# Feed-forward stage: product M4 issued three matmuls later, and the next block's preparation in smaller pieces

## The chip, the cores and the metric

The kernel runs on one core of one Trainium2 chip. The metric is the device time of one execution, in microseconds (us). Before the change the median of three runs is 5206.62 us (5202.1 to 5209.15).

## What is computed

Three layers, each on the output of the one before, in float32. The change touches the last one alone, the feed-forward layer with d_model 256 and d_ff 2048, on 24576 rows:

```python
def _attn_ref(u, v, z):            # 8 batches, 3072 rows, 256 columns
    scores = (1.0 / S) * np.matmul(z, z.transpose(0, 2, 1))
    return u * np.matmul(np.maximum(scores, 0.0) ** 2, v)
...
    x = _moe_ref(x=attn_out.reshape(B * S, D), **moe_kwargs)   # top-1 of 8 experts
...
def _moe2_ref(x, w_in, w_out):
    h = x @ w_in                               # 24576 x 2048
    g = h * (1.0 / (1.0 + np.exp(-h)))
    return (g @ w_out).astype(np.float32)      # 24576 x 256
```

## The kernel before

The program has two pipelines one after the other: `pipeline_ab` (attention and experts, up to about 3190 us) and `pipeline_c` (feed-forward, from there to the end). All orders are written out by hand: within the stage each engine runs its instructions in the order in which Python emits them, and waits only for semaphores.

**Blocks and steps.** `pipeline_c` (L1253 and on) goes through 24 blocks of 1024 rows (CB), each in two halves of 512 rows. A block has 8 steps (GP), one per 2 x 128 hidden columns, so there are 192 steps, numbered g; i = g mod 8 is the step's place in its block. Every float32 product is three matmuls of 128x512 (high by high, high by low, low by high part), emitted by `emit_M` (L1211 to L1213) and `emit_AV_c` (L1237 to L1239).

**One step.** The four quarters H11, H12, H21, H22 of the hidden layer (two column groups by two row halves) are made from seven products M1 to M7 instead of eight, in PSUM banks Q (two, alternating by step), R and Z:
- M1 goes to Q, M2 to R; H11 = Q + R.
- M6 is added onto Q (start=False), so Q must have been copied out first (`copy(0)` before M6, `copy(1)` before M5, `copy(2)` before M3; ScalarE, L1269).
- M7 starts Z; H22 = Z + copy 2.
- M4 is added onto Z, so it must wait until VectorE has read Z for H22 (`add("H22", 2, Z)`, L1272); H21 = Z + copy 1.
- M3 is the last product on Q; H12 is Q itself.

Each quarter then goes through `sig` (ScalarE, L1275, sigmoid), `mul` (VectorE, L1278), `high` (ScalarE, L1284, rounded copy) and `low_part` (VectorE, L1288, the rest), and one step later through `emit_AV_c`, six matmuls with the second weight (three for each of d = 0, 1) into four accumulators. "H12's six matmuls" below means that last part for H12. Some of this falls into the next step: mul H21, high H21 and high H12, and the low parts of H22, H12 and H21.

**TensorE's order in a step** is M1, M2, H11's six, M6, M7, H22's six, M5, H21's six, M3, M4, H12's six: 45 matmuls, where the six-matmul groups belong to the step before.

**VectorE's order** is low H22, low H12, mul H21 (all three of the step before), add H11, low H21, mul H11, the preparation, low H11, add H22, mul H22, add H21, mul H12. **ScalarE's order** is high H12 of the step before, copy 0, high H21, sig H11, copy 1, high H11, the preparation, copy 2, sig H22, sig H12, high H22, sig H21.

**Preparation of the next block.** `prep_c(b)` (L1190) lists what makes the inputs of block b: `load_c` (eight DMAs on SP's queue), two `tr_c` (VectorE transposes of 128x1024, L1158), four `sum_c` (VectorE, 128x512, L1173) and four `parts_c`, each a split: a ScalarE copy (`xp`, L153) and a VectorE subtraction that waits for it (L154), 128x1024 for three of them and 128x512 for the fourth. Before the change one entry of the list is emitted in the middle of each step: the load at i=1, both transposes at i=2, two sums at i=3, two at i=4, the three large splits at i=5, 6 and 7, the small split at i=0 of the block itself.

**Output.** At i=0 the accumulators of the block before are read by four VectorE transposes (`evac_c`, L1245), each pair followed by four stores on SP's queue.

Of the kernel before, what the change touches and what calls it, by code (L numbers as in the profile page):

```python
# [20 lines left out]
def relu2_attention__moe_top1__silu_ffn_kernel(  # L21
# [60 lines left out]
    NCB = N // CB  # L82
    GP = DFF // P // 2
# [874 lines left out]
    for b in range(NBLK):  # L958
        g = NIT + b * FP
# [191 lines left out]
    def load_c(b):  # L1151
        for t in range(2):
            XC[t] = mt("y", [P, CH // 32, 64], F32, "xc", t)
            load_rows(XC[t], CH // P, X2[b * CB + t * CH:b * CB + (t + 1) * CH])

    def tr_c(b, t):
        o = TC[t] = mt("u", [P, KD, CH], F32, "xs", t)
        V.transpose(out=o.rearrange("p k (j c) -> p j k c", c=32),  # L1158
                    in_=XC[t].rearrange("p j (r k) -> p j k r", k=KD))

    def sum_c(n):

        if n == 0:
            TC[2] = mt("y", [P, KD, CH], F32, "xs", 0)
            o, x, y = TC[2][:, 0], TC[1][:, 0], TC[0][:, 0]
        elif n == 1:
            o, x, y = TC[1][:, 0], TC[1][:, 1], TC[1][:, 0]
        elif n == 2:
            o, x, y = TC[2][:, 1], TC[1][:, 1], TC[2][:, 0]
        else:  # L1170
            TC[3] = mt("y", [P, CH], F32, "xs", 1)
            o, x, y = TC[3], TC[0][:, 1], TC[2][:, 1]
        V.tensor_tensor(out=o, in0=x, in1=y, op=ALU.subtract)  # L1173

    def parts_c(b, n):

        if n == 3:
            h, l = (mt("st", [P, CH], F32R, "xp", x) for x in range(2))
        elif n == 1:
            h, l = (mt("a" if b % 2 == 0 else "xh", [P, KD, CH], F32R, "xp") for x in range(2))  # L1180
        else:
            h, l = (mt("w2" if n else "xl", [P, KD, CH], F32R, "xp", 2 * (n and b % 2) + x) for x in range(2))
        split(h, l, TC[n])
        if n == 3:
            XF["T4"] = h, l
        else:
            for k, name in enumerate((("B11", "B21"), ("T3", "B22"), ("T1", "T2"))[n]):
                XF[b % 2 if n else 0, name] = h[:, k], l[:, k]

    def prep_c(b):  # L1190

        return [[], [lambda: load_c(b)], [lambda: tr_c(b, 0), lambda: tr_c(b, 1)],
                [lambda: sum_c(0), lambda: sum_c(1)], [lambda: sum_c(2), lambda: sum_c(3)],
                [lambda: parts_c(b, 1)], [lambda: parts_c(b, 2)], [lambda: parts_c(b, 0)], [lambda: parts_c(b, 3)]]

    FACTORS = dict(M1=("A11", "B11"), M2=("A12", "B21"), M3=("S4", "B22"), M4=("A22", "T4"), M5=("S1", "T1"),
                   M6=("S2", "T2"), M7=("S3", "T3"))
# [8 lines left out]
    def emit_M(g, name, o, start=True):  # L1206
        b, i = divmod(g, GP)
        w, x = FACTORS[name]
        wh, wl = (a[:, i * P:(i + 1) * P] for a in weights_c(w))
        xh, xl = XF[x if x == "T4" else (0 if x in ("B11", "B21") else b % 2, x)]  # L1210
        T.matmul(o, lhsT=wh, rhs=xh, start=start, stop=False, skip_group_check=True)  # L1211
        T.matmul(o, lhsT=wh, rhs=xl, start=False, stop=False, skip_group_check=True)  # L1212
        T.matmul(o, lhsT=wl, rhs=xh, start=False, stop=True, skip_group_check=True)  # L1213

    QUADS = dict(H11=(0, 0), H22=(1, 1), H21=(1, 0), H12=(0, 1))
    quads, acc_c, out_c, room = {}, {}, {}, {}
# [5 lines left out]
        room["c"] = [*(mt("st", [P, CH], F32, "c", 6 + i) for i in range(2)), x[:, 0]]  # L1222
        room["a"] = {q: mt("st", [P, CH], F32, "sg", 2 + i) for i, q in enumerate(QUADS)}

    def emit_AV_c(g, q):

        b, i = divmod(g, GP)
        f, t = QUADS[q]
        x = quads.pop((g, q))
        start = i == 0 and q in ("H11", "H22")  # L1230
        stop = i == GP - 1 and q in ("H21", "H12")
        for d in range(2):
            if start:
                acc_c[b, d, t] = cw["ps"].tile([P, CH], F32, tag=f"acc{2 * t + d}", name="acc", bufs=1)
            o = acc_c[b, d, t]
            wh, wl = (cw["o"][:, f * GP + i, y, d * P:(d + 1) * P] for y in range(2))
            T.matmul(o, lhsT=wh, rhs=x[:, 0], start=start, stop=False)  # L1237
            T.matmul(o, lhsT=wh, rhs=x[:, 1], start=False, stop=False)  # L1238
            T.matmul(o, lhsT=wl, rhs=x[:, 0], start=False, stop=stop)  # L1239

    def evac_c(b, t, d):
        if d == 0:
            out_c[t] = mt("u", [P, CH // 32, 64], F32, "oc", t)
        o = out_c[t]
        V.transpose(out=o.rearrange("p j (r k) -> p j k r", k=2)[:, :, d],  # L1245
                    in_=acc_c.pop((b, d, t)).rearrange("p (j c) -> p j c", c=32))
        if d == 1:
            rows = out[b * CB + t * CH:b * CB + (t + 1) * CH]
            for i in range(4):
                SP.dma_start(out=rows[:, 64 * i:64 * i + 64].rearrange("(j c) m -> c j m", c=32),  # L1250
                             in_=o[32 * i:32 * i + 32])

    def pipeline_c():  # L1253
        not_c.close()
        ps = cw["ps"] = ctx.enter_context(tc.tile_pool(name="psC", bufs=1, space=PSUM))
        banks = [ps.tile([P, CH], F32, tag=f"m{i}", name="m", bufs=1) for i in range(4)]
        ns = NCB * GP
        rooms_c()
        n_quad = 0
        H, C, S = room["H"], room["c"], room["a"]  # L1260
        for g in range(ns + 1):
            now, old = g < ns, g > 0
            b, i = divmod(g, GP)
            end = old and i == 0
            todo = prep_c(b)[GP] if now and i == 0 else prep_c(b + 1)[i] if now and b + 1 < NCB else []
            Q, R, Z = banks[g % 2], banks[2], banks[3]

            def copy(n, src):
                A.activation(out=C[n], in_=src, func=AF.Copy)  # L1269

            def add(q, n, src):
                V.tensor_tensor(out=H[q], in0=src, in1=C[n], op=ALU.add)  # L1272

            def sig(q, src=None):
                A.activation(out=S[q], in_=H[q] if src is None else src, func=AF.Sigmoid)  # L1275

            def mul(q, src=None):
                V.tensor_tensor(out=S[q], in0=H[q] if src is None else src, in1=S[q], op=ALU.mult)  # L1278

            def high(g, q):  # L1280
                nonlocal n_quad
                quads[g, q] = mt("hl"[n_quad % 2], [P, 2, CH], F32R, "g")
                n_quad += 1
                A.activation(out=quads[g, q][:, 0], in_=S[q], func=AF.Copy)  # L1284

            def low_part(g, q):
                x = quads[g, q]
                V.tensor_tensor(out=x[:, 1], in0=S[q], in1=x[:, 0].bitcast(F32), op=ALU.subtract)  # L1288

            if now:  # L1290
                emit_M(g, "M1", Q)
            if old:
                high(g - 1, "H12")
                low_part(g - 1, "H22")
            if now:
                copy(0, Q)
                emit_M(g, "M2", R)
            if old:
                low_part(g - 1, "H12")
                mul("H21")  # L1300
                high(g - 1, "H21")
            if now:
                add("H11", 0, R)
            if old:
                low_part(g - 1, "H21")
                emit_AV_c(g - 1, "H11")
            if now:
                sig("H11")
                mul("H11")
                emit_M(g, "M6", Q, False)  # L1310
                copy(1, Q)
                high(g, "H11")
                emit_M(g, "M7", Z)
            for fn in todo:
                fn()
            if now:
                low_part(g, "H11")
            if old:
                emit_AV_c(g - 1, "H22")
            if now:  # L1320
                emit_M(g, "M5", Q, False)
                copy(2, Q)
            if old:
                emit_AV_c(g - 1, "H21")
            if now:
                add("H22", 2, Z)
                sig("H22")
                emit_M(g, "M3", Q, False)
                emit_M(g, "M4", Z, False)
            if end:  # L1330
                evac_c(b - 1, 0, 0)
            if now:
                sig("H12", Q)
                mul("H22")
                high(g, "H22")
            if end:
                evac_c(b - 1, 0, 1)
            if now:
                add("H21", 1, Z)
                mul("H12", Q)  # L1340
                sig("H21")
            if old:
                emit_AV_c(g - 1, "H12")
            if end:
                for d in range(2):
                    evac_c(b - 1, 1, d)

    with tc.manual_schedule():
        start_a()
# [48 lines left out]
```

## Time and profile before

| | |
|---|---|
| median of 3 runs | 5206.62 us (5202.1 to 5209.15) |
| the profiled execution's own time | 5207.61 us |
| its span, first to last instruction | 5205.9 us |
| busy over the span: TensorE, VectorE, ScalarE, GpSimd | 99%, 77%, 67%, 15% |
| feed-forward stage | from about 3198 us to the end |
| granted TensorE clock, mean | 0.996 of full |

All timeline rows are of one execution and give the start and duration of an instruction, and in brackets how long its engine stood idle just before it and what ended that. TensorE's matmuls overlap: each is shown 0.39 us long, but in an undisturbed stretch the next one begins about 0.227 us after the one before, so the busy share says little, and gaps are read from starts. The profiled execution is 1.0 us above the median of the runs.

### The profile page before, as it was taken

The page shows a single profiled execution, that of the slowest core. Times are in us where ns is not written, and L with a number is a line of the kernel's source. Part 1 is how long each engine was busy: PE and PEld are TensorE (multiplying, and loading weights), DVE is VectorE, ACT ScalarE, POOL GpSimd, SP SyncE. Part 2 cuts the span into 40 slices and gives each one's busy share as a digit, 9 for nine tenths or more (in the row PEclk, how much of TensorE's full clock was granted, in tenths as well). Part 3 has the DMA queues.
Part 4 walks back from the last instruction along what each step waited for, and adds up shares of the span by engine and source line. Part 5 has one row for each costly group of instructions (what it writes and reads, how often), then busy time and mean ns, then how long its engine had stood idle before and what let it go on. Part 6 is the DMA issues. An engine that isn't in the chain of part 4 may idle for free.

```text
span 5205.9 us, 76118 instructions
## 1 busy us (share of the span) xinstructions
PE 5130.2 (99%) x27488; PEld 4403.7 (85%) x27488; DVE 4016.5 (77%) x5760; ACT 3501.9 (67%) x5213; POOL 759.3 (15%) x977
## 2 busy tenths in 40 slices
PE   8999999999999999999999998999999999999999
PEld 7999888888989898888888887888888888888887
DVE  6687777777777778778877667888887888888787
ACT  7787777777777776555555555666666666666666
POOL 1131313131323221311111111000000000000000
PEclk9999999999999999999999999999999999999999
DMA  4555555556565556755555543011010101101010
GB/s 150 179 169 177 175 181 166 180 168 190 166 179 166 181 168 191 192 161 159 162 153 154 162 141 115 21 28 33 17 33 17 33 21 29 33 17 33 17 33 17
DMA packets 789371, 594.31 MB, mean 114 GB/s; under 512 B 473692, under 2 KB 706175, under 8 KB 788992
## 3 DMA queue, kind: packets, MB, share of 16 engines
q1 hardware_dynamic: 616960, 464.93, 30.2%
q10 hardware_dynamic: 152928, 73.95, 5.6%
q0 software_dynamic: 19104, 50.56, 2.6%
q8 instruction: 215, 3.52, 0.3%
q14 instruction: 164, 1.34, 0.1%
HBM read 368.03 MB, written 210.73 MB: 111 GB/s over the span
## 4 chain that ended last, share of the span: by engine, by line
PE 68%; issue 9%; DVE 8%; ACT 8%; DMA 6%; POOL 1%; SPq 1%; ACTq 0%; POOLq 0%; DVEq 0%
PE acc L244 6%; PE acc L241 6%; PE acc L1239 5%; PE acc L1237 5%; PE acc L1238 5%; PE m L1211 4%; PE m L1213 4%; PE m L1212 4%; PE acct L702 4%; PE acct L703 4%; PE acct L704 4%; PE acc L243 3%; PE acc L242 3%; ACT g L1284 2%; PE s L647 2%
## 5 line engine op out<-in xcount | busy, mean ns | idle before, releaser
L1284 ACT ACTIVATE g<-sg 128x512 fp32r<-128x512 f32 x768 | 485.8, 633 | 222.5 <-DVE sg L1278 209.3
L1237 PE MATMUL acc<-g,wo 128*128 128x512 f32 x1536 | 598.5, 390 | 0.0
L1238 PE MATMUL acc<-g,wo 128*128 128x512 f32 x1536 | 597.9, 389 | 0.2 <-DVE g L1288 0.2
L1239 PE MATMUL acc<-g,wo 128*128 128x512 f32 x1536 | 597.9, 389 | 0.0
L1288 DVE TENSOR_TENSOR g<-sg,g 128x512 fp32r<-128x512 f32 x768 | 524.5, 685 | 58.0 <-ACT g L1284 22.0
L702 PE MATMUL acct<-vs,th 128*128 128x256 f32 x1920 | 542.7, 283 | 5.5 <-DVE rt L509 5.5
L703 PE MATMUL acct<-vs,th 128*128 128x256 f32 x1920 | 542.3, 282 | 0.0
L704 PE MATMUL acct<-vs,tl 128*128 128x256 f32 x1920 | 542.1, 282 | 0.0
L244 PE MATMUL acc<-vs,ah 128*128 128x512 f32 x1344 | 533.3, 397 | 0.0
L241 PE MATMUL acc<-vs,ah 128*128 128x512 f32 x1344 | 532.8, 396 | 0.0
L1275 ACT ACTIVATE sg<-hs 128x512 f32<-128x512 f32 x576 | 364.4, 633 | 216.0 <-DVE hs L1272 206.7
L669 DVE TENSOR_TENSOR al<-a,ah 128x1024 fp32r<-128x1024 f32 x336 | 409.9, 1220 | 108.2 <-ACT ah L662 108.0
L1278 DVE TENSOR_TENSOR sg<-hs,sg 128x512 f32<-128x512 f32 x576 | 395.6, 687 | 120.4 <-ACT sg L1275 118.6
L656 ACT ACTIVATE a<-s 128x1024 f32<-128x1024 f32 x336 | 342.2, 1018 | 183.8 <-PE s L648 160.6
L932 ACT ACTIVATE hh<-hps 128x1024 fp32r<-128x1024 f32 (+1 forms) x220 | 213.7, 971 | 348.4 <-PE hps L918 344.1
L933 DVE SCALAR_TENSOR_TENSOR hl<-hps,hh 128x1024 fp32r<-128x1024 f32 (+1 forms) x220 | 254.0, 1155 | 208.1 <-ACT hh L932 207.5
L681 ACT ACTIVATE th<-at 128x1024 fp32r<-128x1024 f32 x240 | 253.4, 1056 | 224.3 <-PE acct L703 139.7
L667 DVE STREAM_TRANSPOSE tb<-a 128x1024 f32<-128x1024 f32 x240 | 297.5, 1240 | 128.5 <-ACT a L658 125.0
L243 PE MATMUL acc<-vs,al 128*128 128x256 f32 x1344 | 375.4, 279 | 0.0
L703 PEld LDWEIGHTS acct<-vs,th 128*128 128x128 f32 x1920 | 366.1, 191 | 10.4
L242 PE MATMUL acc<-vs,al 128*128 128x256 f32 x1344 | 374.0, 278 | 0.0
L702 PEld LDWEIGHTS acct<-vs,th 128*128 128x128 f32 x1920 | 365.4, 190 | 7.8 <-DVE rt L509 7.8
(246 smaller groups left out, 13978.7 us busy)
## 6 DMA issues: line engine op xcount, KB each, us to landing
ts_scratch<-tb SPq DMA_DIRECT2D x240, 512.0 KB, 3.4
at<-ts_scratch SPq DMA_DIRECT2D x960, 128.0 KB, 2.8
r<-in_moe_w_dram SPq DMA_DIRECT2D x220, 512.0 KB, 5.0
vr<-in_v_dram ACTq DMA_DIRECT2D x48, 512.0 KB, 4.8
ut<-in_u_dram ACTq DMA_DIRECT2D x48, 512.0 KB, 4.5
xb<-xs_scratch SPq DMA_DIRECT2D x192, 128.0 KB, 2.6
xc<-x_scratch SPq DMA_DIRECT2D x192, 128.0 KB, 2.5
out_dram<-oc SPq DMA_DIRECT2D x192, 128.0 KB, 2.0
```

Source lines behind the costliest of these rows:

```text
L241: T.matmul(acc, lhsT=hs[0], rhs=ws[0], start=start, stop=False)
L242: T.matmul(acc[:, D:2 * D], lhsT=ls[0], rhs=ws[0][:, 0:D], start=False, stop=False)
L243: T.matmul(acc[:, D:2 * D], lhsT=ls[1], rhs=ws[1][:, 0:D], start=False, stop=False)
L244: T.matmul(acc, lhsT=hs[1], rhs=ws[1], start=False, stop=stop)
L702: T.matmul(acc[:, kk], lhsT=lh, rhs=vq[:, 0], start=(q == 0), stop=False)
L703: T.matmul(acc[:, kk], lhsT=lh, rhs=vq[:, 1], start=False, stop=False)
L704: T.matmul(acc[:, kk], lhsT=ll, rhs=vq[:, 0], start=False, stop=(q == QT - 1))
L1237: T.matmul(o, lhsT=wh, rhs=x[:, 0], start=start, stop=False)
L1238: T.matmul(o, lhsT=wh, rhs=x[:, 1], start=False, stop=False)
L1239: T.matmul(o, lhsT=wl, rhs=x[:, 0], start=False, stop=stop)
L1284: A.activation(out=quads[g, q][:, 0], in_=S[q], func=AF.Copy)
L1288: V.tensor_tensor(out=x[:, 1], in0=S[q], in1=x[:, 0].bitcast(F32), op=ALU.subtract)
```

## The change

M4 moves behind the first three of H12's six matmuls; `emit_AV_c` gets an argument `half` for that. On VectorE mul H12 now stands ahead of add H21. The preparation list gets two entries a step: the even one at the old place in the middle of the step, the odd one at the step's end. The load of a block's input goes to i=0 of the block before it.

```diff
     def prep_c(b):
-        return [[], [lambda: load_c(b)], [lambda: tr_c(b, 0), lambda: tr_c(b, 1)],
-                [lambda: sum_c(0), lambda: sum_c(1)], [lambda: sum_c(2), lambda: sum_c(3)],
-                [lambda: parts_c(b, 1)], [lambda: parts_c(b, 2)], [lambda: parts_c(b, 0)], [lambda: parts_c(b, 3)]]
+        none = lambda: None
+        return [none, none, lambda: tr_c(b, 0), none, lambda: tr_c(b, 1), none, lambda: sum_c(0), lambda: sum_c(1),
+                lambda: sum_c(2), lambda: sum_c(3), lambda: parts_c(b, 1), none, lambda: parts_c(b, 2), none,
+                lambda: parts_c(b, 0), none, lambda: parts_c(b, 3)]
...
-    def emit_AV_c(g, q):
+    def emit_AV_c(g, q, half=None):
...
-        x = quads.pop((g, q))
+        x = quads[g, q] if half == 0 else quads.pop((g, q))
...
-        for d in range(2):
+        for d in range(2) if half is None else (half,):
...
-            for fn in todo:
-                fn()
+            if now and i == 0:
+                prep_c(b)[2 * GP]()
+                if later:
+                    load_c(b + 1)
+            if later:
+                prep_c(b + 1)[2 * i]()
...
                 emit_M(g, "M3", Q, False)
+            if old:
+                emit_AV_c(g - 1, "H12", 0)
+            if now:
                 emit_M(g, "M4", Z, False)
...
             if now:
+                mul("H12", Q)
                 add("H21", 1, Z)
-                mul("H12", Q)
                 sig("H21")
             if old:
-                emit_AV_c(g - 1, "H12")
+                emit_AV_c(g - 1, "H12", 1)
             if end:
                 for d in range(2):
                     evac_c(b - 1, 1, d)
+            if later:
+                prep_c(b + 1)[2 * i + 1]()
```

The line numbers of the changed kernel are one higher than before from L1211 on. The following rows are each engine's own order around the end of step i=5 and the start of i=6 of one block. Names: sg_35720, 35721, 35722, 35723 hold H11, H22, H21 and H12 after sigmoid; m_35715 is Z, m_35712 and m_35713 are the two Q; c_35718 and c_35719 are copy 0 and copy 1; hs_35716 holds copy 2 and then H21.

VectorE before, from low H11 of step 5 to low H21 in step 6:

```order
L1288 TENSOR_TENSOR g_49787<-sg_35720,g_49787 128x512
L1272 TENSOR_TENSOR hs_35717<-m_35715,hs_35716 128x512
L1278 TENSOR_TENSOR sg_35721<-hs_35717,sg_35721 128x512
L1272 TENSOR_TENSOR hs_35716<-m_35715,c_35719 128x512
L1278 TENSOR_TENSOR sg_35723<-m_35713,sg_35723 128x512
L1288 TENSOR_TENSOR g_49823<-sg_35721,g_49823 128x512
L1288 TENSOR_TENSOR g_49837<-sg_35723,g_49837 128x512
L1278 TENSOR_TENSOR sg_35722<-hs_35716,sg_35722 128x512
L1272 TENSOR_TENSOR hs_35717<-m_35714,c_35718 128x512
L1288 TENSOR_TENSOR g_49846<-sg_35722,g_49846 128x512
```

VectorE after, the same piece:

```order
L1289 TENSOR_TENSOR g_49787<-sg_35720,g_49787 128x512
L1273 TENSOR_TENSOR hs_35717<-m_35715,hs_35716 128x512
L1279 TENSOR_TENSOR sg_35721<-hs_35717,sg_35721 128x512
L1279 TENSOR_TENSOR sg_35723<-m_35713,sg_35723 128x512
L1273 TENSOR_TENSOR hs_35716<-m_35715,c_35719 128x512
L1289 TENSOR_TENSOR g_49826<-sg_35721,g_49826 128x512
L1289 TENSOR_TENSOR g_49837<-sg_35723,g_49837 128x512
L1279 TENSOR_TENSOR sg_35722<-hs_35716,sg_35722 128x512
L1273 TENSOR_TENSOR hs_35717<-m_35714,c_35718 128x512
L1289 TENSOR_TENSOR g_49846<-sg_35722,g_49846 128x512
```

Rows four and five changed places: mul H12 (sg_35723) is now ahead of add H21 (hs_35716); nothing else moved there.

ScalarE after, from copy 2 of step 6 to high H21 in step 7, the same as before but for line numbers and buffer names:

```order
L1270 ACTIVATE hs_35716<-m_35712 128x512
L1276 ACTIVATE sg_35721<-hs_35717 128x512
L1276 ACTIVATE sg_35723<-m_35712 128x512
L1285 ACTIVATE g_49901<-sg_35721 128x512
L1276 ACTIVATE sg_35722<-hs_35716 128x512
L1285 ACTIVATE g_49912<-sg_35723 128x512
L1270 ACTIVATE c_35718<-m_35713 128x512
L1285 ACTIVATE g_49921<-sg_35722 128x512
```

Here nothing moved: sig H21 (sg_35722) still stands ahead of high H12 (g from sg_35723), and copy 0 of the next step behind both.

TensorE before, from the last of H21's matmuls to M1 of the next step, one step:

```order
L1239 MATMUL acc_50093<-g_50444,wo_24244 128x512
L1211 MATMUL m_35712<-xp_49792,s4_35601 128x512
L1212 MATMUL m_35712<-xp_49793,s4_35601 128x512
L1213 MATMUL m_35712<-xp_49792,s4_35602 128x512
L1211 MATMUL m_35715<-xp_50017,wih_24242 128x512
L1212 MATMUL m_35715<-xp_50018,wih_24242 128x512
L1213 MATMUL m_35715<-xp_50017,wil_24243 128x512
L1237 MATMUL acc_50109<-g_50435,wo_24244 128x512
L1238 MATMUL acc_50109<-g_50435,wo_24244 128x512
L1239 MATMUL acc_50109<-g_50435,wo_24244 128x512
L1237 MATMUL acc_50113<-g_50435,wo_24244 128x512
```

TensorE after, the same piece:

```order
L1240 MATMUL acc_50093<-g_50444,wo_24244 128x512
L1212 MATMUL m_35712<-xp_49792,s4_35601 128x512
L1213 MATMUL m_35712<-xp_49793,s4_35601 128x512
L1214 MATMUL m_35712<-xp_49792,s4_35602 128x512
L1238 MATMUL acc_50109<-g_50435,wo_24244 128x512
L1239 MATMUL acc_50109<-g_50435,wo_24244 128x512
L1240 MATMUL acc_50109<-g_50435,wo_24244 128x512
L1212 MATMUL m_35715<-xp_50017,wih_24242 128x512
L1213 MATMUL m_35715<-xp_50018,wih_24242 128x512
L1214 MATMUL m_35715<-xp_50017,wil_24243 128x512
L1238 MATMUL acc_50113<-g_50435,wo_24244 128x512
```

M4, the three matmuls into m_35715 (Z), now follows the first three of H12's six matmuls instead of M3 (into m_35712).

## Rows read from the trace of the kernel before

**Rows 1.** Waits, whole feed-forward stage: who waited for whom: us in total, times, longest.
```profile
PEld m L1211 <- DVE hs L1272: 35.1, 70, 0.9
```

**Rows 2.** Timeline of TensorE: M3 to M4 at i=5 and 6; M5 at i=1.
```profile
4009.29 0.39 PE L1213 MATMUL m<-xp,s 128*128 128x512 f32 x1
4009.61 0.50 PE L1211 MATMUL m<-xp,wih 128*128 128x512 f32 x1
4009.94 0.39 PE L1212 MATMUL m<-xp,wih 128*128 128x512 f32 x1
...
4019.73 0.39 PE L1213 MATMUL m<-xp,s 128*128 128x512 f32 x1
4020.26 0.50 PE L1211 MATMUL m<-xp,wih 128*128 128x512 f32 x1
...
4048.51 0.39 PE L1239 MATMUL acc<-g,wo 128*128 128x512 f32 x1
4048.78 0.50 PE L1211 MATMUL m<-xp,wih 128*128 128x512 f32 x1
```

**Rows 3.** Timeline of VectorE, i=3, 4 and 5 of the next block.
```profile
4070.88 0.69 DVE L1272 TENSOR_TENSOR hs<-m,hs 128x512 f32<-128x512 f32 x1 [0.96 <-ACT hs L1269]
...
4081.08 0.69 DVE L1272 TENSOR_TENSOR hs<-m,hs 128x512 f32<-128x512 f32 x1 [0.96 <-ACT hs L1269]
...
4083.11 0.69 DVE L1272 TENSOR_TENSOR hs<-m,c 128x512 f32<-128x512 f32 x1
...
4091.78 0.68 DVE L1272 TENSOR_TENSOR hs<-m,hs 128x512 f32<-128x512 f32 x1
```

**Rows 4.** Timeline of VectorE, add H22 of i=5 to add H22 of i=0.
```profile
4008.87 0.68 DVE L1272 TENSOR_TENSOR hs<-m,hs 128x512 f32<-128x512 f32 x1
4010.25 0.69 DVE L1278 TENSOR_TENSOR sg<-hs,sg 128x512 f32<-128x512 f32 x1 [0.70 <-ACT sg L1275]
4010.86 0.68 DVE L1272 TENSOR_TENSOR hs<-m,c 128x512 f32<-128x512 f32 x1
4011.46 0.68 DVE L1278 TENSOR_TENSOR sg<-m,sg 128x512 f32<-128x512 f32 x1
4012.05 1.47 DVE L1288 TENSOR_TENSOR g<-sg,g 128x512 fp32r<-128x512 f32 x2
...
4019.52 0.68 DVE L1272 TENSOR_TENSOR hs<-m,hs 128x512 f32<-128x512 f32 x1
...
4030.17 0.68 DVE L1272 TENSOR_TENSOR hs<-m,hs 128x512 f32<-128x512 f32 x1
...
4039.25 0.68 DVE L1288 TENSOR_TENSOR g<-sg,g 128x512 fp32r<-128x512 f32 x1
4040.10 0.69 DVE L1272 TENSOR_TENSOR hs<-m,hs 128x512 f32<-128x512 f32 x1 [0.17 <-ACT hs L1269]
```

**Rows 5.** Timeline of ScalarE: sig H21, high H12, copy 0 after i=5; high H12 after i=4.
```profile
4011.63 0.63 ACT L1275 ACTIVATE sg<-hs 128x512 f32<-128x512 f32 x1
4012.17 0.63 ACT L1284 ACTIVATE g<-sg 128x512 fp32r<-128x512 f32 x1
4012.71 0.58 ACT L1269 ACTIVATE c<-m 128x512 f32<-128x512 f32 x1
...
4084.44 0.63 ACT L1284 ACTIVATE g<-sg 128x512 fp32r<-128x512 f32 x1
```

**Rows 6.** Timeline of VectorE, i=2: the two transposes of the preparation.
```profile
4057.71 2.36 DVE L1158 STREAM_TRANSPOSE xs<-xc 128x1024 f32<-128x1024 f32 x2
```

**Rows 7.** The page's DMA issues: operation, count, size of each, us from issue to landing.
```profile
xc<-x_scratch SPq DMA_DIRECT2D x192, 128.0 KB, 2.5
out_dram<-oc SPq DMA_DIRECT2D x192, 128.0 KB, 2.0
```

**Rows 8.** Windows: busy us (count) of PE, PEld, DVE, ACT, POOL; PEclk; DMA share, GB/s.
```profile
3197.90:3210.00 12.10, 6.49 (x13) 3.90 (x14) 8.71 (x10) 4.03 (x7) 0.00 (x0) 0.52 0.07 17
...
4007.25:4089.92 82.67, 82.38 (x360) 67.07 (x359) 67.16 (x102) 55.73 (x92) 0.00 (x0) 1.00 0.11 26
```

More of the change, by code (lines that the diff above doesn't have):

```diff
@@ L1264, in pipeline_c @@
             end = old and i == 0
-            todo = prep_c(b)[GP] if now and i == 0 else prep_c(b + 1)[i] if now and b + 1 < NCB else []
+            later = now and b + 1 < NCB
             Q, R, Z = banks[g % 2], banks[2], banks[3]
```

## The prediction, made before the changed kernel was run

> **What bounds the kernel now.** I began with the page's busy shares (TensorE 99%) and the waits of the feed-forward stage, the only stage that the change touches. There one entry stops TensorE again and again: a weight load of the first matmul of a product waits for VectorE's add, 70 times, 35.1 us in all [rows 1]. 70 is three for each of 23 blocks, and one.
>
> Then the timeline of TensorE. Its undisturbed spacing is 0.227 us, so a step of 45 matmuls takes 10.20 us; the same 10.20 lies between the add H22 of i=3 and of i=4 (4070.88 to 4081.08), both of which wait 0.96 us for copy 2, thus for TensorE's M5 [rows 3]. A block, taken from the add H22 of i=5 to the next one (4008.87 to 4091.78), is 82.91 us [rows 3, 4]. Eight undisturbed steps are 81.60, so 1.31 us a block are lost. The reader finds them in four places [rows 2]: M4 at i=5 begins 0.32 us after M3's last matmul (0.09 late), and the matmul behind it follows at 0.33 instead of 0.227, a restart of 0.11: 0.20 together. At i=6 the gap is 0.53, so 0.30 and 0.11; i=7 is the same. M5 at i=1 begins 0.27 after its predecessor: 0.05 and 0.11. Sum 1.19; the rest is in hundredths.
>
> Last, what holds M4: add H22, which must read bank Z first. From i=5 to i=6 and from i=6 to i=7 the add H22 are 10.65 us apart (4008.87, 4019.52, 4030.17), and none waits for TensorE [rows 4]. That is **a loop of VectorE and ScalarE**, longer than TensorE's 10.20: add H22, sig H22, mul H22, add H21, mul H12, high H12, low H12, mul H21, add H11, sig H11, mul H11, high H11, the split, low H11, add H22. The large split exists at i=5, 6 and 7 only, and there M4 waits 0.45 longer each step. So M4's lateness is no fixed one: it grows by the step, and what matters is whether the change shortens the loop.
>
> **The change part by part.**
>
> *mul H12 ahead of add H21.* Before, mul H22 starts at 4010.25, add H21 at 4010.86, mul H12 at 4011.46, ending at 4012.14 [rows 4]; ScalarE runs sig H21 at 4011.63 and is free for high H12 at 4012.17, exactly when mul H12 is done [rows 5]. Now mul H12 takes 4010.86 and add H21 4011.46, ending at 4012.14. M4 does not hold add H21 there: it starts 0.06 after add H22's end (4009.55 to 4009.61) and is through some 1 us later [rows 2, 4]. ScalarE still has sig H21 ahead of high H12, so sig H21 starts at 4012.17 and high H12 one ScalarE interval later. That interval is 0.54 (4012.17 to 4012.71, high H12 to copy 0) [rows 5]. Everything behind high H12 in the loop moves by 0.54: **the loop becomes 11.19 us**. mul H12 comes earlier for nothing, as its reader on ScalarE stands behind sig H21. The bounds of this term are 0.54 and the instruction's whole duration, 0.63; I take the spacing, since both run back to back.
>
> *M4 three matmuls later* gives it 0.68 us (3 x 0.227). That is a cushion once a block, not once a step, as the loop above shows. It is used up at i=5: in the quiet step i=4 add H21 (4083.11 before) waits for M4 and moves by up to 0.68 to 4083.79; it ends 0.69 later, then 0.03 and sig H21's 0.54, so high H12 starts at 4085.05 instead of 4084.44 [rows 3, 5], 0.61 later (0.54 if M4 is not what add H21 waits for). M4 at i=5 was 0.09 late; now 0.09 + 0.61 - 0.68 = 0.02. I count no loss at i=5; with a restart it would be 0.13.
>
> *Now the sum from i=5 on.* M4 starts 0.74 after add H22's start (4008.87 to 4009.61). Two loops bring add H22 of i=7: 22.38. From there to low H11 of i=0, with the small split, it was 9.08 (4030.17 to 4039.25), so add H22 could have followed 0.61 later, 9.69, but waited for copy 2 until 9.93 [rows 4]. With 0.54 more it comes at 10.23, and TensorE is no longer what it waits for. From add H22 at i=0 to M5 at i=1 it was 8.68 (4040.10 to 4048.78) [rows 2, 4]; I leave that, since there VectorE has the two last output transposes to do while sig H21 and high H12 run. So M5 at i=1 comes 22.38 + 10.23 + 8.68 - 0.74 = 40.55 us after M4 of i=5. TensorE undisturbed needs three steps and 30 matmuls, 30.60 + 6.80 = 37.40. The loss is 3.15, and 0.11 for the last restart: **3.26 a block**. The same count for before: from add H22 at i=5 (4008.87) to M5 at i=1 (4048.78) 39.91, less 0.74 is 39.17, against 30.60 + 33 x 0.227 = 38.09; with the 0.09 at i=5 and the last 0.11 that makes 1.28, where 1.31 was measured. The change costs 3.26 - 1.28 = 1.98 us a block.
>
> *New waits inside that sum.* Copy 0 stands behind high H12, so M6, which needs copy 0, becomes late: counted from add H22, mul H22 +1.38, mul H12 +1.99, add H21 +2.59, its end +3.27, sig H21 +3.30, high H12 +3.84, copy 0 +4.38 to +4.96, while TensorE reaches M6 at 0.74 + 0.79 + 0.68 + 1.36 + 1.36 = 4.93. M6 waits about 0.1 and restarts. It adds nothing where the loop sets the step.
>
> *The smaller pieces.* The three large splits stay whole and in their place; only a transpose and two sums move. The transpose (half of 2.36, 1.18) [rows 6] goes from i=2 to i=1, behind mul H11, where VectorE waits for high H11 anyway; what is left over delays add H22 and is covered by M4's 0.68. Sum 1 and sum 3 (0.61 each, VectorE's spacing in rows 4) go to the ends of i=3 and 4: add H21, the sum and low H22 end 1.82 after add H21's start, while high H12 ends 0.69 + 0.03 + 0.54 + 0.63 = 1.89 after it. Cover 0.07; without it up to 0.61 a block. The load's eight DMAs of 2.5 us now stand on SP's queue ahead of the eight stores of 2.0 us [rows 7]; both have almost a step until a transpose needs them. Cost nothing.
>
> *A rule against it.* The block with four waits had its clock granted at 1.00, and only the stage's start, with TensorE busy for 6.49 of 12.10 us, shows 0.52 [rows 8]; so I price no clock. The Trainium skill, TensorE: Matmul & The Clock Gate, section "A second HAM failure mode: psum-queue depth-cycling", says that many short idles between matmul groups that cycle through PSUM banks can make the clock swing between half and full rate; by that rule more waits would cost far more than their length, and this trace does not bear it out so far.
>
> **Sum.** The preparation runs 23 times, so 23 x 1.98 = 45.5 us. The profiled execution took 5207.6, 1.0 above the median; from the median it is 5206.6 + 45.5, about **5252 us**. By the bounds: 1.5 a block (if VectorE's wait for copy 2 returns and the restarts fall away) gives 5241; 2.6 (0.13 at i=5, 0.09 on each loop, half of sum 3 uncovered) gives 5266.
>
> **Rivals.** What a measurement can tell from no change is 0.2%, 10 us.
> - *Faster: M4's lateness is one of its own place.* If high H12 were not behind sig H21, the loop would not grow, and 0.68 would cover 0.20, 0.42 and 0.42: 1.04 x 23 = 24, so 5183 us. It decides at a loop of 10.20. Against it: two loops of 10.65 in a row, and ScalarE's unchanged order. 6%.
> - *No change: the swap is hidden.* The loop stays 10.65 because low H22 and the wait for high H12 overlap otherwise than I think. Then i=5 gains 0.20, i=6 and 7 keep 0.45, and M5 at i=1, which TensorE reaches 0.68 earlier, waits some 0.5 more: +0.3 x 23 = 7, 5214 us. 6%.
> - *Slower by the clock.* A step at 0.52 takes 19.6 us; four such steps a block, 4 x 9.4 x 23 = 865 us, 6072 us. 2%. It is what the Trainium skill's page TensorE: Matmul & The Clock Gate would lead to, by the section named above.
>
> **The numbers.** My forecast has 86%. Slower: 86 + 2 = 88%; within 0.2%: 6%; faster: 6%. The likeliest case's own range is 5241 to 5266; with a little for what I can't see on either side I give 5236 to 5267, which leaves out the rivals (14%).
>
> **What would show it.** Right: add H22 at i=5, 6, 7 are 11.2 us apart; on ScalarE sig H21 begins when high H12 did, and high H12 0.54 later; M4 waits at i=6 and 7 but not at i=5; a new wait of M6 for copy 0; M5 at i=1 (with M6 ahead of it) loses about 1 us; blocks of 84.9 us; clock 1.00. Wrong: 10.65 or less between those adds, or M4 without waits at i=6 and 7.

## The result and the profile after

The changed kernel takes 5259.71 us (median of 4 runs, 5257.48 to 5263.08) against 5204.36 for the kernel before (4 runs, 5200.85 to 5209.15): a ratio of 1.0106, 95% interval 1.0092 to 1.0120. It is 1.1% slower. The forecast was 5252 us and slower; the measured time lies inside the range.

The profiled execution of the changed kernel took 5257.48 us, 49.9 more than the one before (5207.61). First its waits of the feed-forward stage (who waited for whom: us in total, times, longest), the longest and those of TensorE:

```profile
ACT sg L1276 <- DVE hs L1273: 395.7, 385, 2.0
...
DVE g L1289 <- ACT g L1285: 89.5, 131, 1.0
...
PEld m L1212 <- ACT c L1270: 59.8, 118, 5.4
...
PEld m L1212 <- DVE hs L1273: 43.1, 70, 0.9
...
PEld m L1212 <- ACT hs L1270: 14.5, 47, 1.4
```

And of the kernel before, TensorE's wait for the same copies:

```profile
PEld m L1211 <- ACT c L1269: 13.9, 26, 5.3
```

M4's wait for add H22, 35.1 us and 70 times in [rows 1], has not gone; it is 43.1 us, again 70 times. The waits for ScalarE's copies have grown from 26 (nearly all M5 at i=1) to 118: M6 now waits for copy 0 too. M3 waits for copy 2 47 times, where it was once. VectorE's low parts (L1289), low H12 among them, wait 89.5 us in all for ScalarE's high copies, L1285.

Next VectorE in the changed kernel: add H22 of i=4; then from add H22 of i=5 to add H22 of i=6, with mul H22, mul H12, add H21, low H22 and low H12 between (start, duration, operation, idle before and what ended it); then add H22 of i=7, of i=0 and, in the last row, of i=5 of the next block:

```profile
4016.90 0.69 DVE L1273 TENSOR_TENSOR hs<-m,hs 128x512 f32<-128x512 f32 x1 [0.84 <-ACT hs L1270]
...
4028.26 0.68 DVE L1273 TENSOR_TENSOR hs<-m,hs 128x512 f32<-128x512 f32 x1
4029.64 0.69 DVE L1279 TENSOR_TENSOR sg<-hs,sg 128x512 f32<-128x512 f32 x1 [0.70 <-ACT sg L1276]
4030.25 0.68 DVE L1279 TENSOR_TENSOR sg<-m,sg 128x512 f32<-128x512 f32 x1
4030.85 0.68 DVE L1273 TENSOR_TENSOR hs<-m,c 128x512 f32<-128x512 f32 x1
4031.45 0.68 DVE L1289 TENSOR_TENSOR g<-sg,g 128x512 fp32r<-128x512 f32 x1
4032.81 0.69 DVE L1289 TENSOR_TENSOR g<-sg,g 128x512 fp32r<-128x512 f32 x1 [0.68 <-ACT g L1285]
...
4039.49 0.68 DVE L1273 TENSOR_TENSOR hs<-m,hs 128x512 f32<-128x512 f32 x1
...
4050.72 0.68 DVE L1273 TENSOR_TENSOR hs<-m,hs 128x512 f32<-128x512 f32 x1
...
4060.98 0.68 DVE L1273 TENSOR_TENSOR hs<-m,hs 128x512 f32<-128x512 f32 x1
...
4113.33 0.68 DVE L1273 TENSOR_TENSOR hs<-m,hs 128x512 f32<-128x512 f32 x1
```

The adds are 11.23 us apart (4028.26, 4039.49, 4050.72), where [rows 4] had 10.65. The new piece is the bracket before 4032.81: VectorE stands idle 0.68 us until high H12 is done. ScalarE over the same time, high H12 of i=4 and then sig H22 and, after sig H12, high H22, sig H21, high H12 and copy 0:

```profile
4020.93 0.62 ACT L1285 ACTIVATE g<-sg 128x512 fp32r<-128x512 f32 x1
...
4028.98 0.63 ACT L1276 ACTIVATE sg<-hs 128x512 f32<-128x512 f32 x1 [1.91 <-DVE hs L1273]
...
4030.37 0.63 ACT L1285 ACTIVATE g<-sg 128x512 fp32r<-128x512 f32 x1 [0.27 <-DVE sg L1279]
4031.63 0.63 ACT L1276 ACTIVATE sg<-hs 128x512 f32<-128x512 f32 x1 [0.62 <-DVE hs L1273]
4032.16 0.62 ACT L1285 ACTIVATE g<-sg 128x512 fp32r<-128x512 f32 x1
4032.68 0.58 ACT L1270 ACTIVATE c<-m 128x512 f32<-128x512 f32 x1
```

mul H12 was done at 4030.93, and high H12, which reads it, begins at 4032.16: it stood behind sig H21, for which ScalarE waited 0.62 us. In [rows 5] that order was harmless: sig H21 had started at 4011.63, and high H12 could follow it at 4012.17, just after mul H12's end at 4012.14. On TensorE the M4 of i=5 and 6 (each with the matmul ahead of it and the one behind it), M4 of i=7 and, in the last two rows, M6 and M5 of i=1:

```profile
4028.71 0.39 PE L1240 MATMUL acc<-g,wo 128*128 128x512 f32 x1
4029.00 0.50 PE L1212 MATMUL m<-xp,wih 128*128 128x512 f32 x1
4029.34 0.39 PE L1213 MATMUL m<-xp,wih 128*128 128x512 f32 x1
...
4039.51 0.40 PE L1240 MATMUL acc<-g,wo 128*128 128x512 f32 x1
4040.23 0.50 PE L1212 MATMUL m<-xp,wih 128*128 128x512 f32 x1 [0.32 <-DVE hs L1273]
4040.56 0.39 PE L1213 MATMUL m<-xp,wih 128*128 128x512 f32 x1
...
4051.46 0.50 PE L1212 MATMUL m<-xp,wih 128*128 128x512 f32 x1 [0.31 <-DVE hs L1273]
...
4066.64 0.50 PE L1212 MATMUL m<-xp,s 128*128 128x512 f32 x1 [0.36 <-ACT c L1270]
...
4069.66 0.50 PE L1212 MATMUL m<-xp,wih 128*128 128x512 f32 x1
```

M4 at i=6 begins 0.72 us after the matmul ahead of it, where [rows 2] had 0.53, though it stands three matmuls later. At i=5 the gap is 0.29, hardly less than the 0.32 of [rows 2]. The block as a whole (windows: length, busy us of PE, PEld, DVE, ACT, POOL, granted clock, DMA share, GB/s):

```profile
4028.20:4113.30 85.10, 84.12 (x361) 66.80 (x361) 67.27 (x103) 54.15 (x92) 0.00 (x0) 1.00 0.11 25
```

From add H22 of i=5 to the same add of the next block it is 85.07 us (4028.26 to 4113.33), where it was 82.91: 2.16 more, and 23 x 2.16 = 49.7, all that the two profiled executions differ by. VectorE and ScalarE have about the work of [rows 8], 67.27 and 54.15 us a block (67.16 and 55.73 before); their waits are what grew. The clock is 1.00.

### The profile page after: what moved, and what is told of

It is laid out like the page before. It is cut to its first block, busy times and chain, and to the rows that moved or that the text cites. A ratio compares the mean times of both kernels' runs of the same rounds, so it can differ in the third digit from the quotient of the medians.

```text
span 5255.8 us, 76335 instructions
## 1 busy us (share of the span) xinstructions
PE 5162.9 (98%) x27488; PEld 4392.6 (84%) x27488; DVE 4016.3 (76%) x5760; ACT 3464.2 (66%) x5213; POOL 757.9 (14%) x977
## 4 chain that ended last, share of the span: by engine, by line
PE 58%; DVE 14%; ACT 11%; issue 10%; DMA 6%; POOL 1%; SPq 1%; ACTq 0%; POOLq 0%; DVEq 0%
PE acc L244 6%; PE acc L241 6%; DVE sg L1279 5%; PE acct L702 4%; PE acct L703 4%; PE acct L704 4%; ACT g L1285 3%; PE acc L243 3%; PE acc L242 3%; ACT sg L1276 3%; PE m L1212 3%; PE acc L1239 3%; PE acc L1238 3%; PE acc L1240 3%; DVE hs L1273 3%
## 5 line engine op out<-in xcount | busy, mean ns | idle before, releaser
L1285 ACT ACTIVATE g<-sg 128x512 fp32r<-128x512 f32 x768 | 482.6, 628 | 268.6 <-DVE sg L1279 260.3
L1289 DVE TENSOR_TENSOR g<-sg,g 128x512 fp32r<-128x512 f32 x768 | 524.4, 685 | 116.3 <-ACT g L1285 89.5
```

## Experiments

Three theories were set against each other first. A: the swap of mul H12 and add H21 costs, as it puts sig H21 into a loop of VectorE and ScalarE that sets the pace. B: M4's later place costs, by making add H21 and all behind it 0.68 us later. C: the sums at the ends of steps cost. The change was taken apart into its three edits. Each run stands beside runs of the kernel before on the same chip.

**The swap alone**, on the kernel before:

```diff
-                add("H21", 1, Z)
                 mul("H12", Q)
+                add("H21", 1, Z)
                 sig("H21")
```

> The kernel before, with mul H12 put ahead of add H21 on VectorE and nothing else changed. Theory A (the swap puts sig H21 into the loop of VectorE and ScalarE): the add H22 of i=5, 6 and 7 are about 11.2 us apart instead of 10.65, M4 waits longer at all three, a block takes about 85.0 us instead of 82.92, the time is 23 x 2.0 = 46 us longer, 5240 to 5262 us. Theory B (M4's later place costs, since add H21 and all behind it come 0.68 us later) and theory C (the sums at the ends of steps cost): no change, 5200 to 5210 us.

Measured: 5258.76 us against 5203.02, ratio 1.0106 (1.0089 to 1.0123). VectorE's add H22 of i=5, 6 and 7 in this kernel:

```profile
4029.09 0.69 DVE L1272 TENSOR_TENSOR hs<-m,hs 128x512 f32<-128x512 f32 x1
...
4040.33 0.69 DVE L1272 TENSOR_TENSOR hs<-m,hs 128x512 f32<-128x512 f32 x1
...
4051.56 0.69 DVE L1272 TENSOR_TENSOR hs<-m,hs 128x512 f32<-128x512 f32 x1
```

11.24 and 11.23 us apart, and M4 begins 0.91, 1.09 and 1.08 us after the matmul ahead of it ([rows 2]: 0.32 and 0.53): this one line alone gives the loop and the whole loss. B and C fall as explanations of the 55 us.

**M4's place alone**, on the kernel before:

```diff
                 emit_M(g, "M3", Q, False)
-                emit_M(g, "M4", Z, False)
+            if old:
+                emit_AV_c(g - 1, "H12", 0)
+            if now:
+                emit_M(g, "M4", Z, False)
...
-                emit_AV_c(g - 1, "H12")
+                emit_AV_c(g - 1, "H12", 1)
```

> The kernel before, with M4 alone moved behind the first half of H12's matmuls; VectorE's order as before. Theory A: the loop stays at 10.65, M4 at i=6 and 7 still waits, and M5 at i=1 is reached earlier and waits some 0.5 us more; 0.3 to 0.5 us a block, 5211 to 5217 us. Theory B: nearly the whole loss, 5240 to 5262 us. Theory C: no change.

Measured: 5215.53 us, ratio 1.0023 (1.0013 to 1.0032). TensorE's waits for add H22 (M4's, which the move was to cover) and for the copies:

```profile
PEld m L1211 <- DVE hs L1272: 35.3, 70, 0.9
PEld m L1211 <- ACT c L1269: 24.4, 26, 5.4
```

M4's wait is 35.3 us in 70 waits, as in [rows 1] (35.1): the move gave nothing, not even at i=5. VectorE shows why, by add H22 and add H21 of i=4 and add H22 of i=5; below it M4 of i=5 and the matmul ahead of it:

```profile
4002.89 0.69 DVE L1272 TENSOR_TENSOR hs<-m,hs 128x512 f32<-128x512 f32 x1 [0.29 <-ACT hs L1269]
...
4005.60 0.69 DVE L1272 TENSOR_TENSOR hs<-m,c 128x512 f32<-128x512 f32 x1 [0.62 <-PE m L1213]
...
4014.26 0.68 DVE L1272 TENSOR_TENSOR hs<-m,hs 128x512 f32<-128x512 f32 x1
```

```profile
4014.69 0.39 PE L1239 MATMUL acc<-g,wo 128*128 128x512 f32 x1
4015.00 0.50 PE L1211 MATMUL m<-xp,wih 128*128 128x512 f32 x1
```

Add H21 of i=4, which reads what M4 wrote, now waits 0.62 us for the later M4, and add H22 of i=5 comes 11.37 us after that of i=4 instead of 10.70 ([rows 3]). So M4 at i=5 begins 0.31 us after the matmul ahead of it, as before (0.32). The copies' wait (M5 at i=1) is 24.4 us and was 13.9: M5 of i=1 begins 0.72 us after the matmul ahead of it instead of 0.27. That 0.45 is what a block is longer, 83.37 instead of 82.92 us. Alone, M4's place costs 12 us, and in the way that theory B names.

**The pieces alone**, on the kernel before: `prep_c` and its calls as in the change, nothing else.

> The kernel before, with the preparation in the new places alone (load at i=0, one transpose at i=1 and one at i=2, a sum in the middle and one at the end of i=3 and i=4). Theory A: the sum at the end of i=4 has no wait to hide in, since high H12 is not late, so M4 at i=5 is up to 0.4 us later; nothing else moves; 0.3 to 0.4 us a block, 5212 to 5215 us. Theory B: no change, 5200 to 5210. Theory C: 5240 to 5262 us.

Measured: 5212.89 us, ratio 1.0022 (1.0012 to 1.0031). The pieces cost 10 us, in the place that was named: M4's wait rose to 44.5 us, in the same 70 waits, and M4 of i=5 begins 0.72 us after the matmul ahead of it (4007.49), 0.40 more than in [rows 2], while i=6 and 7 have 0.53 and 0.55 as before.

```profile
PEld m L1212 <- DVE hs L1273: 44.5, 70, 0.9
```

```profile
4008.21 0.50 PE L1212 MATMUL m<-xp,wih 128*128 128x512 f32 x1 [0.34 <-DVE hs L1273]
```

**The changed kernel with the swap undone**: add H21 put back ahead of mul H12.

> The changed kernel, with add H21 put back ahead of mul H12; M4's new place and the preparation's new places are kept. Theory A: add H22 at i=5, 6 and 7 are 10.65 us apart again, and most of the loss is gone; what stays is the sum of the two runs with one part each, 0.6 to 0.9 us a block, 5218 to 5227 us. Theories B and C: the loss stays, 5255 to 5262 us.

Measured: 5227.81 us, ratio 1.0048 (1.0031 to 1.0065). The loop is 10.65 again, and what is left, 24.8 us, is the 12.5 and 9.9 of the two single parts and 2.4 more; the time is 0.8 us above the expected range. So some 31 of the change's 55 us go with one line undone.

**The changed kernel with the pieces undone**: the preparation in its old places, the other two edits kept.

> The changed kernel, with the preparation back in its old places (M4 later and mul H12 ahead are kept). Theory A: sum 3 at the end of i=4 runs in the wait for high H12 that the swap makes, so taking it away changes little, 85.0 to 85.1 us a block, 5250 to 5260 us. If the pieces cost by themselves also here what they cost alone, 10 us, it is 5245 to 5250 us.

Measured: 5257.57 us against 5203.77, ratio 1.0101 (1.0084 to 1.0118), as slow as the changed kernel. The parts don't add up: alone they cost 55.7, 12.5 and 9.9 us, which would be 78, and the change with all three costs 55. Once low H12 has to wait for high H12 (0.68 us at i=4 in this run, which has no sum there), sum 3 with its 0.61 us runs inside that wait. M4's later place hides too: from add H22 of i=4 to that of i=5 it is 11.29 us with the swap alone, 11.37 with M4 alone and 11.37 in this run, which has both (10.70 before). With mul H12 ahead, add H21 comes later anyway, and little is left of its wait for M4.

**High H12 ahead of sig H21.** If the order on ScalarE is the cause, it can be mended there, with the swap kept:

```diff
             if old:
-                high(g - 1, "H12")
                 low_part(g - 1, "H22")
...
                 mul("H12", Q)
                 add("H21", 1, Z)
+                high(g, "H12")
                 sig("H21")
```

> The changed kernel, with high H12 moved on ScalarE ahead of sig H21, from the start of the next step to the end of its own; VectorE's and TensorE's orders stay as changed. Theory A (high H12 stands behind sig H21): high H12 starts when mul H12 ends, low H12 no longer waits, VectorE goes from mul H22 to mul H21 in five spacings of 0.605, 3.03 instead of 3.19 us before, so the loop is about 10.5 us, M4 at i=5 doesn't wait, and i=6 and 7 lose 0.3 each: 82.7 to 82.9 us a block, 5196 to 5204 us, the time of the kernel before or a little less. Theory D (mul H12 in front costs because it holds VectorE up until M3 is done): ScalarE's order changes nothing, 5255 to 5262 us.

Measured: 5198.50 us against 5203.77, ratio 0.9989 (0.9980 to 0.9999). The loss is gone. ScalarE runs high H22 and high H12 without a gap and sig H21 behind them, and VectorE goes from mul H22 through mul H12 and add H21 to the two low parts without a wait:

```profile
4006.12 1.23 ACT L1285 ACTIVATE g<-sg 128x512 fp32r<-128x512 f32 x2 [0.27 <-DVE sg L1279]
4007.38 0.63 ACT L1276 ACTIVATE sg<-hs 128x512 f32<-128x512 f32 x1
```

```profile
4004.01 0.68 DVE L1273 TENSOR_TENSOR hs<-m,hs 128x512 f32<-128x512 f32 x1
4005.39 0.69 DVE L1279 TENSOR_TENSOR sg<-hs,sg 128x512 f32<-128x512 f32 x1 [0.70 <-ACT sg L1276]
4006.00 0.68 DVE L1279 TENSOR_TENSOR sg<-m,sg 128x512 f32<-128x512 f32 x1
4006.60 0.68 DVE L1273 TENSOR_TENSOR hs<-m,c 128x512 f32<-128x512 f32 x1
4007.20 1.28 DVE L1289 TENSOR_TENSOR g<-sg,g 128x512 fp32r<-128x512 f32 x2
...
4014.47 0.68 DVE L1273 TENSOR_TENSOR hs<-m,hs 128x512 f32<-128x512 f32 x1
```

The loop is 10.46 us (4004.01 to 4014.47). It was not the swap by itself that cost, but the swap with ScalarE's unchanged order: theory D, that mul H12 in front holds VectorE up, falls. Still 10.46 is more than TensorE's 10.20, so M4 is still late at i=6 and 7, by 0.12 and 0.09 us (a loss of 0.3 each was expected); a block takes 82.58 us, a little under the expected 82.7 to 82.9.

**The large split taken out of the loop.** What makes the loop long at i=5, 6 and 7 is VectorE's 1.65 us of waiting for the split's copy, ahead of low H11 and add H22, here in the kernel before at i=6:

```profile
4017.77 1.23 DVE L154 TENSOR_TENSOR xp<-xs,xp 128x1024 fp32r<-128x1024 f32 x1 [1.65 <-ACT xp L153]
```

On the kernel before, VectorE's half of the split was put where it waits 0.70 us for sig H22 anyway:

```diff
+    rest_c = []
     def parts_c(b, n):
...
-        split(h, l, TC[n])
+        if b and n != 3:
+            x = TC[n]
+            A.activation(out=h, in_=x, func=AF.Copy)
+            rest_c.append(lambda: V.tensor_tensor(out=l, in0=x, in1=h.bitcast(F32), op=ALU.subtract))
+        else:
+            split(h, l, TC[n])
...
                 sig("H22")
+            while rest_c:
+                rest_c.pop()()
+            if now:
```

> The kernel before, with VectorE's half of the three large splits moved from ahead of low H11 to behind add H22, where VectorE stands idle 0.70 us for sig H22. Theory A: the loop loses the wait for the split (low H11 can follow high H11, 2.08 us earlier: 4016.83 instead of 4018.91) and gains 1.14 - 0.70 = 0.44, so it is 10.65 - 2.08 + 0.44 = 9.0 us, under TensorE's 10.20: M4 waits nowhere, only M5 at i=1 still does, a block takes 81.8 us, 23 x 1.1 = 25 us less than before, 5174 to 5182 us. Theory E (VectorE has no room in these steps, the work only moves and mul H22 and what follows come late instead): M4 is free but the waits turn up at M6 or M5, 5195 to 5207 us.

Measured: 5178.72 us (5175.92 to 5181.08) against 5203.77, ratio 0.9948 (0.9931 to 0.9965): faster than both kernels, by 25 us than before and by about 81 than the change. Copy 2 on ScalarE, then add H22, the split's half and mul H22 on VectorE at i=7:

```profile
4014.58 0.60 ACT L1276 ACTIVATE hs<-m 128x512 f32<-128x512 f32 x1 [0.34 <-PE m L1220]
```

```profile
4015.21 0.69 DVE L1279 TENSOR_TENSOR hs<-m,hs 128x512 f32<-128x512 f32 x1 [1.20 <-ACT hs L1276]
4015.82 1.22 DVE L1188 TENSOR_TENSOR xp<-xs,xp 128x1024 fp32r<-128x1024 f32 x1
4016.95 0.69 DVE L1285 TENSOR_TENSOR sg<-hs,sg 128x512 f32<-128x512 f32 x1
```

The brackets show it: add H22 waits 1.20 us for copy 2, and copy 2 for TensorE, where add H22 had waited for nothing in [rows 4]. The adds of i=5, 6 and 7 are 10.20 us apart: TensorE sets the pace again. Its waits for add H22 in the whole stage:

```profile
PEld m L1218 <- DVE hs L1279: 0.9, 1, 0.9
```

One of 70 is left. Theory E, that VectorE has no room for it, falls.

**Both on the changed kernel**: high H12 first and the late half.

> The changed kernel with both edits, high H12 ahead of sig H21 and the late half of the large splits. Theory A: once the loop is under 10.20 the places of M4, mul H12 and the pieces are worth nothing, so this is as fast as the kernel before with the late half alone, 81.8 us a block, 5174 to 5182 us. If M4's later place is worth something by itself, it is faster than that run by over 5 us.

Measured: 5183.32 us (5175.29 to 5185.41), ratio 0.9953 (0.9936 to 0.9969). That is 1 us above the expected range, but a block takes 81.81 us here and in the run before this one, and the intervals overlap: no worth of M4's later place, mul H12 and the pieces shows once the loop is under TensorE's step.

## Why the prediction was right

- **The bound.** Right. That M4's lateness belongs to a loop and not to its place was read from two adds 10.65 us apart that wait for nothing, and the run with M4's place alone shows it: the same 70 waits, the same 35 us, the same gaps at i=5, 6 and 7 (0.31, 0.53, 0.55).
- **mul H12 ahead of add H21.** Right in place and kind: a loop of 11.19 us was forecast, 11.23 measured. The step that fell short is the start of sig H21, taken as 0.03 after add H21's end. It is 0.10 (4030.85 + 0.68 = 4031.53, start 4031.63). The rows of before had that number (add H21 from 4010.86, 0.68 long, sig H21 at 4011.63: 0.09 [rows 4, 5]); the 0.03 came from mul H12 to high H12, but high H12 also began 0.54 after sig H21, which is ScalarE's own spacing, so that it need not have been a wait at all.
- **M4 at i=5.** "I count no loss at i=5" was a term that was mis-sized: M4 begins 0.29 after the matmul ahead, 0.06 late where 0.02 was worked out. High H12 of i=4 comes 4.03 us after add H22 (4016.90 to 4020.93), where it was 3.36 (4081.08 to 4084.44 [rows 3, 5]): 0.67 later and not 0.61, which is the late start of sig H21 again. The restart, counted in "it would be 0.13", doesn't belong in the sum: M4 of i=6 starts 11.23 us after M4 of i=5 (4029.00 to 4040.23), the loop's own length, whatever TensorE loses between. That the cushion of 0.68 is used up before i=5 was right; the rival "no change", which gave i=5 a gain of 0.20, had it wrong, since M4's place alone gave 0.01 there.
- **From add H22 of i=0 to M5 of i=1.** Left at 8.68 in the prediction, and measured as 8.68 (4060.98 to 4069.66), with the wait shared between M6 and M5. From M4 of i=5 to M5 of i=1 it was 40.66 us (4029.00 to 4069.66) against the forecast 40.55; the 0.11 are 0.04 on each of the two loops and 0.03 from add H22 of i=7 to that of i=0 (10.26 for 10.23). The waits of M3 for copy 2 were not foreseen; like those of M6 at i=6, 7 and 0 they add nothing where the loop sets the step.
- **Pieces and DMAs.** "Cost nothing" holds within the change and would have been wrong without the swap: alone the pieces cost 9.9 us. The cover was thin (0.07 us by the working), and the swap itself had made it.
- **The clock.** 1.00 in a block with ten waits of TensorE (235 waits of weight loads for add H22 and the copies, in 23 blocks). The rule of the Trainium skill (TensorE: Matmul & The Clock Gate, "A second HAM failure mode: psum-queue depth-cycling") that many short idles between matmul groups can make the clock swing is not what these waits of up to 0.5 us did here.
- **The sum.** 1.98 us a block was forecast, 2.16 measured: 0.11 of the difference is in the 40.66, 0.06 in M4 at i=5, the rest in hundredths. The medians differ by 55 us, 5 more than the two profiled executions. In these the feed-forward stage, from its first add H22 to its last, grew from 1977.35 to 2027.86 us, so by 50.5. The stage begins earlier or later from one execution to the next (its first add H22 at 3205.8 to 3214.3 us in the ten traces of this document), and single runs of one kernel spread over 5 to 14 us; that the 5 us lie there is likely and not shown.

## What to carry to other kernels

When an engine at 99% waits again and again at one place, look whether what it waits for comes back in a period of its own: two engines at 77% and 67% can form a loop that is longer than the busiest engine's step. Moving the waiting product later then gives nothing a step, and here not even once a block, as the add that reads the product had to wait for it in turn; a reordering on one engine of the loop has to be checked on the other, where an instruction may now stand ready behind one that is not; and what helps is to take a wait out of the loop, here by putting half an operation where its engine stood idle anyway.

## What was not expected of the hardware

- ScalarE's sig H21 begins 0.09 to 0.10 us after VectorE's add H21 ends (4031.53 to 4031.63; in the run with high H12 first 4007.28 to 4007.38), while sig H22 follows add H22's end by 0.04 (4028.94 to 4028.98) and high H22 follows mul H22's by 0.04 (4030.33 to 4030.37). All are waits of the same two engines on 128x512 tiles. Why the one is more than twice as long stays open.
- Behind a matmul that had to wait, the next begins a further 0.11 us late (0.33 to 0.35 us after it instead of 0.227), after a lateness of 0.06 (4029.00 to 4029.34) as after 0.49 (4040.23 to 4040.56); the waiting matmul's own row is 0.50 us long instead of 0.39. Where TensorE sets the pace, a short wait thus costs more than it lasts; where a loop of other engines sets it, the 0.11 is taken up by the next wait.
